# A third landing row, shorter split lead and earlier coefficient loads in the middle of an FNet/H3 kernel

## The chip, the cores and the metric

The kernel runs on one core of a Trainium2 chip. A core has a matrix engine (PE, TensorE), a vector engine (DVE), a scalar engine (ACT), a general engine (POOL) and a sequencer that issues transfers (SP); each runs its own list of instructions in order and waits on semaphores for the others. The metric is the device time of one execution in microseconds.

## The reference, cut to what matters

Two kinds of layers alternate, A, B, A, B, each with a layer norm and a residual, on x of 2048 rows by 576 channels:

```python
def A(x):   # FNet: real part of a Fourier transform along channels and along rows
    a, b = x @ Wd_re.T, x @ Wd_im.T
    return Ws_re @ a - Ws_im @ b

def B(q, k, v, shift_k, ssm_k, ssm_D):   # H3: causal convolution over all 2048 rows
    kv = short_conv4(k, shift_k) * v
    y = irfft(rfft(pad(kv)) * rfft(pad(ssm_k)))[:2048] + kv * ssm_D
    return q * y

x = x + A(layernorm(x)); x = x + B(layernorm(x), ...)
x = x + A(layernorm(x)); x = x + B(layernorm(x), ...)
```

The convolution of B takes k, v and the filter alone and not x, so its result (before the gate) is computed once, beside the first layer A, and used in both layers B.

## The kernel before, in words

All products run in float32 by parts: an operand is split into a rounded high part h (a copy on ACT) and a low part l = x - h (a subtraction on DVE), and a product is h*h + h*l + l*h, three matmuls.

Layer A (`layer`) runs 128 steps n = (g, tb, k): four blocks tb of 512 output rows, two parts g (real, imaginary) and 16 pieces k of 128 input rows. Step n needs one coefficient piece of 128x512 (`c_mat`): a transfer into a raw tile (ring `craw`), then its split into a slot of the ring `cs` of three. A step is 14 matmuls of 512 columns into the five PSUM banks s0 to s3 and rm. After the last k of each 16 steps (n = 47, 63, 79, 95, 111 in the stretch at issue) the banks are evacuated into U: four splits (`evac_u`, L262), and for rm a copy, an addition and a split through a scratch tile `rt` (`evac_r`, L271 to L273). With a block done, four pieces of the hidden product with W (`hidden`, 27 matmuls of 288 columns each half) are pending.

Between these steps, the branch of layer B (`branch`) is fed in small portions. Its middle stage begins at step 45 and has 37 groups: load from t, split (`split_mid`), a product with the filter's and one with the signal's half (`mid_kernel`, `mid_signal`), four DVE operations that multiply them (L570 to L573), a split (`mid_round`) and an inverse product (`mid_inverse`) whose copy is stored to `v_d`. The inverse stage then has 16 rows j of two halves: load of a row from `v_d` (`load_row`), split of each half (`split_row`), a product of four 288-wide matmuls with constants loaded by POOL, and its evacuation by two copies on ACT (L661) and two additions on DVE (L662). ACT operations of both stages show as L510 in the profile, since they go through a helper.

What sets the order: the Python code writes the operations in program order, with a plan that hands out the branch's portions by cost (`MID_COST`, `MID_PAUSE`, `I2_PAUSE`, `I2_COST`; `branch_steps` takes the next portion when the plan's share is behind the work passed). A scheduler in the compiler then fixes each engine's list when the kernel is built, by readiness in a model of its own; `issue_after` pins some pairs. On the chip each list runs strictly in order.

In the middle and inverse stages the ring `craw` has two tiles: the words at `RT_AT`, which are also the scratch `rt` of `evac_r`, and a tile at word 8 of the same buffer. Step 48 is the first to use this ring. Coefficient piece n + 2 is loaded and split at step n. In the inverse stage two rows can be landing (`land`), four half rows can be split (`df`), three half rows are split ahead of the first product, and row j + 2 is loaded when the second half of row j has been split.

Of the kernel before, what the change touches and what calls it, by code (L numbers as in the profile page):

```python
# [10 lines left out]
F32 = mybir.dt.float32  # L11
# [4 lines left out]
P = 128  # L16
Q = P // 2
S = 2048
D = 576
J = S // P  # L20
TB = 4
NT = 512
# [16 lines left out]
MID_LOAD = 45  # L39
MID_FROM = 47  # L40
I2_END = 111
PREP = 113
MW = 504
MID_COST = (2.9, 2.6, 1.8)
MID_PAUSE = 4.0
I2_PAUSE = 6.0
BORDER = {J - 1: 0.5, 0: 0.75}
I2_COST = 2.4
# [20 lines left out]
def fnet_h3_kernel(ctx: ExitStack, tc: tile.TileContext, x, c_mat, w_re, w_im, k_pad, v, shift_k,  # L69
# [144 lines left out]
    CT = {}  # L214

    def load_c(step):
        g, tb, k = step
        raw = ring["craw"]()
        anchor.append(load_after(raw, c_mat[g, tb, k]) if anchor else nc.sync.dma_start(raw, c_mat[g, tb, k]).ins)
        c = ring["cs"]()  # L220
        t = c[:, :NT], c[:, NT:]
        with behind(*stored):
            halved[:] = split(t[0], t[1], raw)
        CT[step] = t

# [88 lines left out]
    def layer(get_x, xres, done, pending, blocks=TB):  # L314
        steps = [(g, tb, k) for tb in range(blocks) for g in range(2) for k in range(J)]
        for n, (g, tb, k) in enumerate(steps):
# [3 lines left out]
            if n + 2 < len(steps):  # L320
                load_c(steps[n + 2])
            for i in range(XLEAD + 1 if blocks == TB else 1):
                if n + i < J:
                    get_x(n + i)
# [7 lines left out]
            for dc in range(NC):  # L332
                xh = X[k][:, dc * P:(dc + 1) * P]
                xl = X[k][:, D + REM + dc * P:D + REM + (dc + 1) * P]
                mm(ps[dc], xh, c[0], first, False)
                mm(ps[dc], xh, c[1], False, False)
                mm(ps[dc], xl, c[0], False, last)
                if dc == NC // 2 - 1:
                    yield n, False
                if last:  # L340
                    (evac_u if blocks == TB else save_u)(g, ps, dc)
# [19 lines left out]
    def branch():  # L361
# [135 lines left out]
        apart = [m1[:, at:at + MW].bitcast(F32), flts[:, 8 + NT:8 + NT + MW]]  # L497
        lay(flts, RT_AT, ("craw", NT, 1))
        at = lay(flts, 8, ("craw", NT, 1)) + MW
# [127 lines left out]
        lay(m1, 0, ("df", 2 * D, 4), ("fc", 2 * P, 6))  # L627
        assert lay(flts, 8 + NT, ("land", 2 * D, 2), ("vo", D, 3)) <= RT_AT - 3 * HD

# [10 lines left out]
        def split_row(j, hf):  # L640
            if j < J:
# [5 lines left out]
                if hf:  # L647
                    del landed[j]
                    load_row(j + 2)
# [20 lines left out]
        for j in range(2):  # L670
            load_row(j)
        yield I2_PAUSE
        for n in range(3):
            split_row(*divmod(n, 2))
            yield I2_COST
        for j in range(J):
            fc, yo = fcs.pop(j), ring["vo"]()
            for hf in range(2):
                vf = halves.pop((j, hf))
                split_row(*divmod(2 * j + hf + 3, 2))  # L680
# [129 lines left out]
    work = mid_work + I2_PAUSE + 35 * I2_COST  # L810
# [386 lines left out]
```

## Time and profile before

| | |
|---|---|
| median of three runs | 1185.95 us (1183.89 to 1187.08) |
| the profiled execution | 1185.81 us |
| its span, first to last instruction | 1184.0 us |
| mean granted PE clock | 0.998 |
| middle stage, from the waits and the timeline | about 218 to 512 us |
| inverse stage | about 516 to 605 us |

In the profile's rows a name like `mats<-flts` says which buffer is written from which: `mats` holds the parts of x and the split coefficients, `flts` float32 tiles (raw coefficients, landing rows, scratch), `mid` the split data of the branch, `u` and `w` the parts of U and W, `bk` the three PSUM banks that the branch and the hidden product share, `s` and `rm` the five banks of layer A. PEld are weight loads, which run beside matmuls; SPq and ACTq are the transfers that SP and ACT issue. In a timeline row stand start, duration, engine, line, operation, tiles, shape and count; in brackets how long the engine had stood idle before it and what ended that.

### The profile page before, as it was taken

The page shows a single profiled execution, that of the slowest core. Times are in us where ns is not written, and L with a number is a line of the kernel's source. Part 1 is how long each engine was busy: PE and PEld are TensorE (multiplying, and loading weights), DVE is VectorE, ACT ScalarE, POOL GpSimd, SP SyncE. Part 2 cuts the span into 40 slices and gives each one's busy share as a digit, 9 for nine tenths or more (in the row PEclk, how much of TensorE's full clock was granted, in tenths as well). Part 3 has the DMA queues.
Part 4 walks back from the last instruction along what each step waited for, and adds up shares of the span by engine and source line. Part 5 has one row for each costly group of instructions (what it writes and reads, how often), then busy time and mean ns, then how long its engine had stood idle before and what let it go on. Part 6 is the DMA issues. An engine that isn't in the chain of part 4 may idle for free.

```text
span 1184.0 us, 17305 instructions
## 1 busy us (share of the span) xinstructions
PE 1166.3 (99%) x6013; PEld 1005.3 (85%) x6013; DVE 846.0 (71%) x1415; ACT 630.8 (53%) x1154; POOL 67.4 (6%) x100
## 2 busy tenths in 40 slices
PE   7999999999999999999999999999999999999997
PEld 6888888887878888888888898888888888889997
DVE  7899794678677678657857765864875776874764
ACT  7965665566655667556646666534434445540200
POOL 2200000000000000001002111000000000001111
PEclk9999999999999999999999999999999999999999
DMA  9889898546666647468857786772682598696621
GB/s 343 289 262 306 275 288 258 193 156 193 192 203 195 200 133 194 108 195 261 248 151 262 244 259 214 253 259 72 205 300 73 179 315 275 197 343 192 214 97 41
DMA packets 153770, 255.60 MB, mean 216 GB/s; under 512 B 27601, under 2 KB 66769, under 8 KB 153682
## 3 DMA queue, kind: packets, MB, share of 16 engines
q1 hardware_dynamic: 115122, 205.58, 54.7%
q10 hardware_dynamic: 33952, 42.63, 10.6%
q0 software_dynamic: 4608, 6.29, 2.2%
q8 instruction: 47, 0.77, 0.3%
q14 instruction: 41, 0.34, 0.1%
HBM read 187.80 MB, written 66.65 MB: 215 GB/s over the span
## 4 chain that ended last, share of the span: by engine, by line
PE 92%; DMA 3%; DVE 2%; ACT 1%; issue 1%; SPq 0%; POOLq 0%; POOL 0%; DVEq 0%; ACTq 0%
PE s L78 53%; PE bk L78 33%; PE rm L78 6%; DMA flts<-in_c_mat 1%; DMA flts<-vd 1%; DVE mats L96 0%; ACT mid L510 0%; DMA vd<-flts 0%; DVE u L96 0%; DVE flts L184 0%; ACT flts L510 0%; DVE mid L645 0%; DVE mats L201 0%; ACT mats L95 0%; DVE flts L662 0%
## 5 line engine op out<-in xcount | busy, mean ns | idle before, releaser
L78 PE MATMUL s<-mats 128*128 128x512 f32 x2088 | 525.9, 392 | 0.7 <-ACT mats L95 0.6
L78 PEld LDWEIGHTS s<-mats 128*128 128x128 f32 x2088 | 387.0, 188 | 79.3 <-ACT mats L95 1.1
L96 DVE TENSOR_TENSOR mats<-flts,mats 128x512 fp32r<-128x512 f32 x201 | 137.4, 688 | 69.9 <-ACT mats L95 67.2
L95 ACT ACTIVATE mats<-flts 128x512 fp32r<-128x512 f32 x201 | 125.8, 627 | 98.6 <-PE bk L78 35.2
L510 ACT ACTIVATE flts<-bk 64x504 f32<-64x504 f32 (+1 forms) x212 | 111.8, 528 | 64.2 <-PE bk L78 59.0
L78 PE MATMUL bk<-w,u 128*128 128x288 f32 x864 | 121.5, 295 | 0.0
L78 PEld LDWEIGHTS bk<-w,u 128*128 128x128 f32 x864 | 118.1, 188 | 2.5 <-DVE flts L295 0.6
L78 PE MATMUL bk<-mid 128*128 128x504 f32 (+1 forms) x461 | 115.9, 366 | 3.4 <-DVE flts L662 1.6
L78 PEld LDWEIGHTS bk<-mid 128*128 128x128 f32 x461 | 80.5, 188 | 23.4 <-DVE flts L662 4.3
L510 ACT ACTIVATE mid<-flts 128x1008 fp32r<-128x1008 f32 (+2 forms) x106 | 75.0, 710 | 43.7 <-DVE flts L573 18.1
L78 PE MATMUL rm<-mats 128*128 128x512 f32 x304 | 94.9, 391 | 0.0
L458 ACT ACTIVATE flts<-bk 128x288 f32<-128x288 f32 x128 | 50.7, 410 | 49.3 <-PE bk L78 48.1
L78 PE MATMUL bk<-f1r 128*128 128x288 f32 x384 | 64.7, 301 | 6.8 <-ACT f1r L95 6.4
L78 PEld LDWEIGHTS bk<-f1r 128*128 128x128 f32 x384 | 59.9, 192 | 13.3 <-ACT f1r L95 6.4
L78 PE MATMUL bk<-mats 128*128 128x288 f32 (+1 forms) x376 | 67.8, 317 | 0.0
L78 PEld LDWEIGHTS rm<-mats 128*128 128x128 f32 x304 | 57.0, 188 | 12.2
L78 PE MATMUL s<-t,mats 128*128 128x512 f32 x264 | 64.9, 389 | 0.0
L295 DVE TENSOR_TENSOR flts<-flts,bk 128x288 f32<-128x288 f32 x48 | 21.8, 453 | 56.2 <-PE bk L78 56.0
L187 POOL TENSOR_TENSOR flts<-flts 128x1 f32<-128x1 f32 x35 | 30.7, 877 | 541.2 <-DVE flts L186 494.6
L515 DVE TENSOR_TENSOR mid<-flts,mid 128x1008 fp32r<-128x1008 f32 (+2 forms) x74 | 58.1, 802 | 4.6 <-ACT mid L510 4.6
L78 PE MATMUL bk<-mats,t 128*128 128x288 f32 (+1 forms) x368 | 59.3, 303 | 0.0
L78 PEld LDWEIGHTS bk<-mats 128*128 128x128 f32 x376 | 55.6, 188 | 3.4
(151 smaller groups left out, 1486.1 us busy)
## 6 DMA issues: line engine op xcount, KB each, us to landing
flts<-in_c_mat SPq DMA_DIRECT2D x148, 256.0 KB, 3.9
ph<-in_c_mat SPq DMA_DIRECT2D x54, 512.0 KB, 4.2
t<-flts ACTq DMA_DIRECT2D x64, 288.0 KB, 4.8
flts<-in_c_mat SPq DMA_DIRECT2D x30, 512.0 KB, 5.6
flts<-vd SPq DMA_DIRECT2D x16, 576.0 KB, 5.0
vd<-flts ACTq DMA_DIRECT2D x36, 252.0 KB, 3.1
flts<-t SPq DMA_DIRECT2D x16, 504.0 KB, 4.1
ud<-ph ACTq DMA_DIRECT2D x12, 512.0 KB, 6.6
```

The lines of the kernel that those rows point to most:

```text
L78: nc.tensor.matmul(ps, lhsT, rhs, start=first, stop=last, skip_group_check=more)
L95: a = nc.scalar.activation(h, src, AF.Copy).ins
L96: return a, nc.vector.tensor_tensor(l, src, h.bitcast(F32), OP.subtract).ins
L187: pows.append(nc.gpsimd.tensor_tensor(rs, ve, mhalf, OP.pow).ins)
L295: added[:] = [nc.vector.tensor_tensor(rows[hf], rows[hf], ps[:, :HD], OP.add).ins]
L458: stored[:] = [nc.scalar.activation(so[:, b, :], ps[:, :HD], AF.Copy).ins]
L510: last_act.append(nc.scalar.activation(*args, **kw).ins)
L515: nc.vector.tensor_tensor(l, src, h.bitcast(F32), OP.subtract)
```

## The change

Inverse stage: a third landing row is taken from the region of the branch's split data, where one of the four half-row slots is given up and the constants move down; three rows are loaded at the start, row j + 3 follows row j, and halves are split two ahead of their product and not three. `I2_PAUSE` goes from 6 to 10, and one `I2_COST` less stands in the plan's work.

Middle and inverse stages (steps 46 to 112): the transfer of a coefficient piece is parted from its split (`fetch_c`), and piece n + 3 is fetched at step n, behind the split of piece n + 2; at the first step of a group of 16 (k = 0) it is fetched in the middle of the step. The two raw tiles change places in the ring: even pieces use the tile at word 8 and odd ones the shared scratch.

```diff
-I2_PAUSE = 6.0
+I2_PAUSE = 10.0
...
-    CT = {}
+    CT, CR = {}, {}
+
+    def fetch_c(step):
+        g, tb, k = step
+        raw = CR[step] = ring["craw"]()
+        anchor.append(load_after(raw, c_mat[g, tb, k]) if anchor else nc.sync.dma_start(raw, c_mat[g, tb, k]).ins)
 
     def load_c(step):
-        g, tb, k = step
-        raw = ring["craw"]()
-        anchor.append(load_after(raw, c_mat[g, tb, k]) if anchor else nc.sync.dma_start(raw, c_mat[g, tb, k]).ins)
+        if step not in CR:
+            fetch_c(step)
+        raw = CR.pop(step)
...
             if n + 2 < len(steps):
                 load_c(steps[n + 2])
+            soon = blocks == TB and MID_LOAD < n < PREP
+            if soon and k > 0:
+                fetch_c(steps[n + 3])
...
                 if dc == NC // 2 - 1:
                     yield n, False
+                    if soon and k == 0:
+                        fetch_c(steps[n + 3])
...
+        at = lay(flts, 8, ("craw", NT, 1)) + MW
         lay(flts, RT_AT, ("craw", NT, 1))
-        at = lay(flts, 8, ("craw", NT, 1)) + MW
...
-        lay(m1, 0, ("df", 2 * D, 4), ("fc", 2 * P, 6))
+        at = lay(m1, 0, ("df", 2 * D, 3), ("fc", 2 * P, 6))
         assert lay(flts, 8 + NT, ("land", 2 * D, 2), ("vo", D, 3)) <= RT_AT - 3 * HD
+        ring["land"].tiles.append(m1[:, at:at + 2 * D].bitcast(F32))
...
-                    load_row(j + 2)
+                    load_row(j + 3)
...
-        for j in range(2):
+        for j in range(3):
             load_row(j)
         yield I2_PAUSE
-        for n in range(3):
+        for n in range(2):
...
-                split_row(*divmod(2 * j + hf + 3, 2))
+                split_row(*divmod(2 * j + hf + 2, 2))
...
-    work = mid_work + I2_PAUSE + 35 * I2_COST
+    work = mid_work + I2_PAUSE + 34 * I2_COST
```

The lists of the engines differ from step 46 to about step 112 alone. Three places show how; line numbers of the changed kernel are 5 to 11 higher than those of the profile. First ACT's list at the evacuation of step 63 (`u_753` is U, `rm_2555` the remainder's bank, `mats_70<-flts_72 128x512` the high part of a coefficient piece, `mid_2078` the branch's split data), before:

```order
L95 ACTIVATE u_753<-s3_69 128x512
L271 ACTIVATE flts_72<-rm_2555 64x512
L95 ACTIVATE u_753<-flts_72 64x512
L510 ACTIVATE mid_2078<-flts_72 128x1008
L510 ACTIVATE flts_72<-bk_3080 128x504
L594 DMA vd_78<-flts_72 128x504
L95 ACTIVATE mats_70<-flts_72 128x512
L510 ACTIVATE mid_2078<-flts_72 128x504
L510 ACTIVATE flts_72<-bk_3096 64x504 x3
L95 ACTIVATE mats_70<-flts_72 128x512 x2
```

and after:

```order
L95 ACTIVATE u_753<-s3_69 128x512
L276 ACTIVATE flts_72<-rm_2555 64x512
L95 ACTIVATE mats_70<-flts_72 128x512
L95 ACTIVATE u_753<-flts_72 64x512
L520 ACTIVATE mid_2078<-flts_72 128x1008
L520 ACTIVATE flts_72<-bk_3080 128x504
L604 DMA vd_78<-flts_72 128x504
L95 ACTIVATE mats_70<-flts_72 128x512
L520 ACTIVATE mid_2078<-flts_72 128x504
L520 ACTIVATE flts_72<-bk_3097 64x504 x3
L95 ACTIVATE mats_70<-flts_72 128x512
```

The split of piece 66 has moved from behind the store of `v_d` to between the copy and the split of the remainder; pieces 67 and 68 stand where 66 and 67 stood. On SP, the loads of 66, 67 and 68 follow each other directly after the change; before, a store of W and a load from t stand between 67 and 68.

Second, PE's list behind step 79, where `rm_3073` is the remainder's bank of step 79 and `rm_4005` that of steps 80 and on, and each `bk` a product of the middle stage, before:

```order
L78 MATMUL rm_3073<-mats_70 128x512 x2
L78 MATMUL bk_3984<-mid_2078 128x504 x3
L78 MATMUL bk_3996<-mid_2078 128x504
L78 MATMUL s0_66<-mats_70 128x512 x2
L78 MATMUL bk_3996<-mid_2078 128x504 x2
L78 MATMUL s0_66<-mats_70 128x512
L78 MATMUL bk_4022<-mid_2078 128x504 x2
L78 MATMUL s1_67<-mats_70 128x512 x3
L78 MATMUL s2_68<-mats_70 128x512 x3
L78 MATMUL s3_69<-mats_70 128x512 x3
L78 MATMUL rm_4005<-mats_70 128x512 x2
```

and after:

```order
L78 MATMUL bk_3997<-mid_2078 128x504 x3
L78 MATMUL s0_66<-mats_70 128x512 x3
L78 MATMUL bk_4014<-mid_2078 128x504 x3
L78 MATMUL s0_66<-mats_70 128x512 x3
L78 MATMUL bk_4039<-mid_2078 128x504 x2
L78 MATMUL s1_67<-mats_70 128x512 x6
L78 MATMUL bk_4039<-mid_2078 128x504
L78 MATMUL s0_66<-mats_70 128x512
L78 MATMUL s1_67<-mats_70 128x512
L78 MATMUL s2_68<-mats_70 128x512 x3
L78 MATMUL s3_69<-mats_70 128x512 x3
L78 MATMUL rm_4005<-mats_70 128x512 x2
```

Parts of steps 81 and 82 (s0 and s1) now stand ahead of s2, s3 and rm of step 80. Behind step 47 the order changes in the same manner: one product moves ahead of step 47's s2, and step 50's first matmul stands behind step 49's s0, ahead of step 48's s1. DVE's list at step 79 now has the four multiplications of one product and a 1008-wide split ahead of the subtractions that evacuate s2 and s3.

Third, ACT's list at the start of the inverse stage, from the copy of step 95's remainder to the first evacuation of an inverse product (`bk_4612`, after the change `bk_4611`; `128x576` is a half row's split, `128x4x72` the last store to `v_d`), before:

```order
L271 ACTIVATE flts_72<-rm_4005 64x512
L95 ACTIVATE u_753<-flts_72 64x512
L510 ACTIVATE mid_2078<-flts_72 128x288
L510 ACTIVATE flts_72<-bk_4499 128x288
L596 DMA vd_78<-flts_72 128x4x72
L95 ACTIVATE mats_70<-flts_72 128x512 x3
L510 ACTIVATE mid_2078<-flts_72 128x576 x4
L95 ACTIVATE mats_70<-flts_72 128x512
L510 ACTIVATE flts_72<-bk_4612 64x288
```

and after:

```order
L276 ACTIVATE flts_72<-rm_4005 64x512
L95 ACTIVATE mats_70<-flts_72 128x512
L95 ACTIVATE u_753<-flts_72 64x512
L520 ACTIVATE flts_72<-bk_4500 128x288
L606 DMA vd_78<-flts_72 128x4x72
L95 ACTIVATE mats_70<-flts_72 128x512 x2
L520 ACTIVATE mid_2078<-flts_72 128x576 x3
L95 ACTIVATE mats_70<-flts_72 128x512
L520 ACTIVATE flts_72<-bk_4611 64x288
```

The last split of the middle stage (`128x288`) has moved ahead of U's evacuation, and three half rows are split before the first inverse product is evacuated, not four. From there on the products stand at the same places in PE's list as before.

## The prediction

> **What bounds the kernel now.** I read the page's engine line first, then the chain that ended last, then windows by stage, then the list of waits, and last the timeline around each wait.
>
> ```profile
> PE 1166.3 (99%) x6013; PEld 1005.3 (85%) x6013; DVE 846.0 (71%) x1415; ACT 630.8 (53%) x1154; POOL 67.4 (6%) x100
> ```
>
> TensorE is the bound, and its only reserve is the stretches where its matmuls do not follow each other at their full pace. The chain gives that pace, from two long stretches with nothing between:
>
> ```profile
> 845.02 23.12 PE s L78 x102
> 1062.17 115.02 PE bk L78 x866
> ```
>
> A 512-wide matmul takes 23.12 / 102 = 0.2267 us from start to start, a 288-wide one 115.02 / 866 = 0.1328 us; the 504-wide ones are close to the first. A later start than that is lost time, even where the busy column says 100%. The windows show where:
>
> ```profile
> 324.00:347.00 23.00, 21.49 (x105) 17.65 (x104) 16.08 (x25) 13.24 (x24) 0.00 (x0) 1.00 0.60 199
> 505.00:552.00 47.00, 45.37 (x247) 38.63 (x246) 31.15 (x54) 27.42 (x52) 3.71 (x7) 1.00 0.75 222
> 850.00:900.00 50.00, 50.00 (x223) 41.40 (x222) 37.17 (x51) 21.07 (x34) 0.00 (x0) 1.00 0.74 245
> ```
>
> (Window, its length, then busy time of PE, weight loads, DVE, ACT, POOL, then the granted clock.) The first is the evacuation at step 63 in the middle stage, the second the start of the inverse stage; the third is a stretch where nothing waits. So few microseconds are to be had. The Trainium skill (Trainium Kernel Development and Optimization, Performance Expectations) says that matmul busy time is a bad measure and weight-load busy share a good one. By that, 85% would leave 15% of the span, 178 us, to be won. The trace does not agree: in the stretch without a wait weight loads are busy 41.40 of 50 us, 83%, so 85% is already full here.
>
> ```profile
> PE bk L78 <- DVE flts L662: 1.6, 3, 0.8
> PE bk L78 <- DVE flts L572: 1.0, 1, 1.0
> ACT mid L510 <- DMA flts<-vd: 12.0, 9, 2.8
> SPq L169 <- DVE u L96: 28.6, 4, 13.1
> ```
>
> (Waiter, what ended the wait, us in all, times, longest.) PE waits for product evacuations of the inverse stage (L662) and of the middle stage (L572). Behind the first stand row loads that land late (ACT waits 12.0 us for them), behind the second the coefficient loads, which stand in SP's queue behind the evacuation of U, because the even steps' raw tile is also the scratch of that evacuation.
>
> **The change, part by part.** No work is added: 128 coefficient loads and splits, 16 row loads, 32 half-row splits, as before. What moves is when loads are issued and in which order ACT, DVE and PE do the same things. I price by place, PE's lost time alone.
>
> *Step 63/64, raw tiles swapped and one step more of lead.*
>
> ```profile
> 330.26 0.81 SPq L169 DMA_DIRECT2D flts<-in_c_mat  x2
> 333.19 0.63 ACT L95 ACTIVATE mats<-flts 128x512 fp32r<-128x512 f32 x1 [2.13 <-DMA flts<-in_c_mat]
> 334.86 0.53 SPq L169 DMA_DIRECT2D flts<-in_c_mat  x1
> 340.46 1.55 PE L78 MATMUL s<-mats 128*128 128x512 f32 x6
> 340.71 0.63 ACT L95 ACTIVATE mats<-flts 128x512 fp32r<-128x512 f32 x1 [4.05 <-PE bk L78]
> 342.48 0.96 PE L78 MATMUL bk<-mid 128*128 128x504 f32 x3 [0.47 <-DVE flts L295]
> 344.48 0.95 PE L78 MATMUL bk<-mid 128*128 128x504 f32 x3 [1.04 <-DVE flts L572]
> 345.27 1.09 PE L78 MATMUL s<-mats 128*128 128x512 f32 x4
> ```
>
> Loads 66 and 67 are issued at 330.26, when the scratch is free; 68 needs 66's split and goes at 334.86; ACT stands 4.05 us until it lands (the wait is put down to PE, but ACT's next work is the split at 340.71). Evacuations behind it come late, and PE loses 342.48 - (340.46 + 6 x 0.2267) = 0.66, then 344.48 - (342.48 + 3 x 0.2267) = 1.32, then 0.11: 2.09 us. After, 66 uses the other tile, is loaded before the evacuation and split inside it, where ACT waits for DVE. 67 takes the shared tile and still goes at about 330.26; SP's later loads and stores queue behind it as they did behind 66. 68 follows at once instead of at 334.86. Even with the 5.85 us that 68 took (334.86 to 340.71) it lands at 336.5; its split then stands at the place in ACT's order where 67's was, at about 336.0. What is late next is a half microsecond on ACT, which PE does not see. Bounds 0 and 2.09; I take 2.1, since the 4.05 us are gone, not just shorter.
>
> *Step 47/48.*
>
> ```profile
> 256.24 1.52 PE L78 MATMUL bk<-mid 128*128 128x504 f32 x6
> 256.93 1.58 ACT L95 ACTIVATE u<-s 128x512 fp32r<-128x512 f32 x3
> 258.53 0.60 ACT L271 ACTIVATE flts<-rm 64x512 f32<-64x512 f32 x1
> 264.68 1.60 PE L78 MATMUL bk<-mid 128*128 128x504 f32 x6
> 266.93 3.01 PE L78 MATMUL s<-mats 128*128 128x512 f32 x12 [0.64 <-ACT mats L95]
> ```
>
> PE loses 266.93 - (264.68 + 6 x 0.2267) = 0.89 us for step 50's split. After, load 50 is early, but PE's new order wants its first matmul much sooner: one product (three matmuls) stands ahead of 256.24, then twelve matmuls follow, so 256.24 + 15 x 0.2267 = 259.64. ACT has by then three U copies (to 258.51), one product copy and the remainder copy (0.60 each) and the split (0.63): 260.34. A new wait of 0.70 takes the place of 0.89. Gain 0.2 (bounds -0.7, if both are paid, and 0.89).
>
> *Step 79/80.* Here nothing is lost before, and the new order mixes middle products into the evacuation (front, second pair of orders).
>
> ```profile
> 438.66 1.06 PE L78 MATMUL bk<-mid 128*128 128x504 f32 x4
> 440.64 1.29 DVE L96 TENSOR_TENSOR u<-s,u 128x512 fp32r<-128x512 f32 x2 [0.35 <-ACT u L95]
> L570 DVE TENSOR_TENSOR flts<-bk,flts 128x504 f32<-128x504 f32 x36 | 24.5, 681 | 22.5 <-PE bk L78 14.6 <-ACT flts L510 7.8
> L515 DVE TENSOR_TENSOR mid<-flts,mid 128x1008 fp32r<-128x1008 f32 x18 | 21.6, 1201 | 0.0
> ```
>
> DVE finishes s3's evacuation at 441.93. After, four product operations (0.68) and a 1008-wide split (1.20) stand ahead of it: 3.9 us later, 445.85. PE wants s3 for step 80 after 26 matmuls from 438.66: 444.55. So up to 1.3 us are lost; none, if DVE's own waits there close up (0.35 in the row). I take the middle, 0.6.
>
> *Inverse stage: three rows landing, splits two ahead, pause 10.*
>
> ```profile
> 509.90 0.44 ACT L510 ACTIVATE mid<-flts 128x288 fp32r<-128x288 f32 x1
> 512.23 0.37 ACTq L596 DMA_DIRECT2D vd<-flts  x1
> 516.32 1.38 SPq L169 DMA_DIRECT2D flts<-vd  x2
> 520.63 1.26 ACT L510 ACTIVATE mid<-flts 128x576 fp32r<-128x576 f32 x2 [2.79 <-DMA flts<-vd]
> 524.35 0.62 PE L78 MATMUL rm<-mats 128*128 128x512 f32 x2
> 525.78 1.02 PE L78 MATMUL bk<-mid 128*128 128x288 f32 x4 [0.80 <-DVE flts L662]
> 526.63 2.16 PE L78 MATMUL bk<-w,u 128*128 128x288 f32 x15
> 528.98 1.03 PE L78 MATMUL bk<-mid 128*128 128x288 f32 x4 [0.19 <-DVE flts L662]
> 544.09 1.55 PE L78 MATMUL s<-mats 128*128 128x512 f32 x6
> 546.29 0.80 PE L78 MATMUL bk<-mid 128*128 128x288 f32 x4 [0.64 <-DVE flts L662]
> ```
>
> PE loses 525.78 - (524.35 + 2 x 0.2267) = 0.98, 526.63 - (525.78 + 4 x 0.1328) = 0.32, 528.98 - (526.63 + 15 x 0.1328) = 0.36 and 546.29 - (544.09 + 6 x 0.2267) = 0.84: 2.50 us. All come from ACT waiting for a row while an evacuation stands behind it. After, the last split of the middle stage (509.90) stands ahead of U's evacuation, and the last product's copy comes straight behind it (third pair of orders): about 509.9 + 0.5, so its store goes some 1.8 us before 512.23, the first rows start and land that much earlier (518.8 instead of 520.63), the third row has its own tile, and each later load is issued five half-rows ahead of its split instead of three. ACT does three splits, not four, before the first evacuation. Bounds: 0 and 2.50; I take 2.5. The pause itself costs PE nothing: it only spaces the plan, whose work goes from 274.1 + 6 + 35 x 2.4 = 364.1 to 274.1 + 10 + 34 x 2.4 = 365.7, so that middle pieces come up to 0.4% sooner. POOL's constant loads now use other words of the same region and wait for the same last middle product.
>
> Sum: 2.1 + 0.2 - 0.6 + 2.5 = 4.2 us. The profiled execution took 1185.81, so 1181.6; the median of the three runs (1185.95) lies 0.1 above it, which I neglect.
>
> **The rivals.**
>
> *Evacuations eat it.* As the 0.70 and 1.3 us above: the new order puts pairs of middle products close together in other places too. With step 80 at 1.3, step 48 at -0.7 and two more such waits of 0.7, the gain is 2.1 + 2.5 - 1.3 - 0.7 - 1.4 = 1.2: 1184.6. For it: step 80 shows what a few DVE operations ahead of an evacuation do. Against: the list of waits has a single PE wait on middle products (L572, 1.0 us), and that is step 64's.
>
> *The earlier fetch does nothing.* There are still two raw tiles, so load n still waits for the split of n-2. Then the inverse stage alone gains, step 80 pays: 1185.8 - 2.5 + 0.6 = 1183.9. Against: at step 64 the tile, not the lead, was the obstacle.
>
> *All waits go.* 2.09 + 0.89 + 2.50 = 5.5 and some tenths at other products: 1180.0.
>
> *Slower: splits two ahead come too late.* One half-row less lies between a split and its product.
>
> ```profile
> 534.87 0.76 DVE L645 TENSOR_TENSOR mid<-flts,mid 128x576 fp32r<-128x576 f32 x1 [0.20 <-ACT mid L510]
> 535.20 0.69 PE L78 MATMUL bk<-mid 128*128 128x288 f32 x4
> 539.49 0.69 PE L78 MATMUL bk<-mid 128*128 128x288 f32 x4
> ```
>
> This split, issued with the product at 535.20, ends at 535.63; after the change its product is the second from there, at 539.49: 3.9 us of margin. If ACT and DVE fall back by more than that, as they would when a row again lands late, products starve as the three above did, 0.73 us each ((0.98 + 0.36 + 0.84) / 3). With 10 of 32: 7.3 us, the 2.5 not gained: 1185.8 - 1.7 + 7.3 = 1191.4. It decides from some seven products on. Against: rows get five half-rows of lead.
>
> **Chances and range.** The forecast (gain 3.6 to 5.2) 0.54, all waits go 0.12, evacuations eat it 0.16, fetch does nothing 0.05, slower 0.13. 1181.6 is the likeliest. About 0.3% (3.6 us) is what a measurement tells here: faster by more 0.66, within 0.21, slower 0.13. The range goes from just below all waits gone, 1179.3, to 1186.0, past the weak gains; it leaves out the slower case and little below. The forecast's own range is 1180.6 to 1182.2.
>
> **What would show it.** Right: no ACT wait near 4 us for a coefficient load around 336 to 341, ACT's wait for rows down from 12.0 to under 4 us, no PE wait on the inverse evacuation, new PE waits under 1 us each near 260 and 445. Wrong: PE waiting for the half-row splits (L645) more than twice, sums of PE waits in the middle stage above 3 us, or rows that still start at 516.

## The result, and the profile after

| | before | after |
|---|---|---|
| median, 7 runs each on one chip | 1186.89 us (1183.89 to 1187.86) | 1181.09 us (1180.28 to 1182.73) |
| profiled execution | 1185.81 us | 1180.65 us |
| its span | 1184.0 us | 1178.8 us |
| mean granted PE clock | 0.998 | 0.999 |

The ratio is 0.9957 with a 95% interval of 0.9946 to 0.9969: 0.43% faster, 3.7 to 6.4 us. The same stages in the windows of the changed kernel (window, length, busy time of PE, weight loads, DVE, ACT, POOL, granted clock, DMA share, GB/s; the second lies 4 us sooner than before, as the stage does):

```profile
324.00:347.00 23.00, 23.00 (x113) 19.48 (x112) 19.07 (x29) 15.48 (x26) 0.00 (x0) 1.00 0.58 192
501.00:548.00 47.00, 47.00 (x260) 41.27 (x259) 31.72 (x54) 28.07 (x53) 4.23 (x8) 1.00 0.76 229
```

PE is busy throughout both, with 113 matmuls in place of 105 and 260 in place of 247. Step 63/64, where ACT had stood for load 68 and three matmul groups had come late, in the timeline of the changed kernel:

```profile
327.50 0.63 ACT L95 ACTIVATE mats<-flts 128x512 fp32r<-128x512 f32 x1
328.34 0.63 ACT L95 ACTIVATE u<-flts 64x512 fp32r<-64x512 f32 x1 [0.21 <-DVE flts L277]
329.78 0.81 SPq L169 DMA_DIRECT2D flts<-in_c_mat  x2
332.62 0.63 ACT L95 ACTIVATE mats<-flts 128x512 fp32r<-128x512 f32 x1 [2.10 <-DMA flts<-in_c_mat]
335.46 0.63 ACT L95 ACTIVATE mats<-flts 128x512 fp32r<-128x512 f32 x1
339.93 1.55 PE L78 MATMUL s<-mats 128*128 128x512 f32 x6
341.31 1.54 PE L78 MATMUL bk<-mid 128*128 128x504 f32 x6
342.69 1.55 PE L78 MATMUL s<-mats 128*128 128x512 f32 x6
```

The split at 327.50 is piece 66's, in the gap in which ACT had waited for DVE; 67 and 68 are issued together at 329.78; 67's split waits 2.10 us as before (2.13), and 68's, at 335.46, waits for nothing. Six matmuls of 0.2267 us take 1.36: 339.93, 341.31, 342.69 follow each other without a gap (1.38 each).

The start of the inverse stage in the same timeline:

```profile
508.02 0.37 ACTq L606 DMA_DIRECT2D vd<-flts  x1
512.17 1.18 SPq L169 DMA_DIRECT2D flts<-vd  x2
514.60 0.52 SPq L169 DMA_DIRECT2D mid<-vd  x1
516.44 1.26 ACT L520 ACTIVATE mid<-flts 128x576 fp32r<-128x576 f32 x2 [3.08 <-DMA flts<-vd]
520.42 0.83 ACT L520 ACTIVATE flts<-bk 64x288 f32<-64x288 f32 x2 [0.69 <-PE bk L78]
521.87 0.62 PE L78 MATMUL rm<-mats 128*128 128x512 f32 x2
522.33 0.69 PE L78 MATMUL bk<-mid 128*128 128x288 f32 x4
```

The last store goes at 508.02 and not 512.23, the rows at 512.17 and not 516.32, and the first evacuation (520.42) now waits for PE and not PE for it. In the list of waits from 205 to 605 us:

```profile
ACT mid L520 <- DMA flts<-vd: 3.3, 2, 3.1
ACT mats L95 <- DMA flts<-in_c_mat: 4.3, 6, 2.1
```

ACT's waits for rows fell from 12.0 us to 3.3. PE waits for no evacuation of L673 (L662 before).

For an account by stage I took PE's lost time from the two traces: for each pair of neighbouring matmuls the time from start to start, less the usual time of the first one's form in these traces (the median: 0.227 us for 512 wide, 0.228 for 504, 0.132 for 288), summed over stretches. The stretches hold the same places in all kernels of this document.

| stretch, us (place) | before | after | gain |
|---|---|---|---|
| 250 to 300 (step 47/48) | 1.71 | 1.43 | 0.28 |
| 300 to 350 (step 63/64) | 2.77 | 0.44 | 2.33 |
| 350 to 500 (step 79/80, rest of the middle stage) | 1.97 | 2.23 | -0.26 |
| 500 to 600 (inverse stage) | 4.50 | 1.31 | 3.19 |
| 600 to 700 (the gate's first rows) | 0.46 | 1.38 | -0.92 |

With 0.12 from all other stretches, where a first matmul that starts 0.69 later is counted in, the sum is 4.74 us, and PE's last matmul does start 4.73 us sooner (1172.15 for 1176.88). The spans differ by 5.2; the rest lies behind the last matmul. The loss of 0.92 stands in no part of the prediction. The orders printed ahead of the prediction were said to differ up to about step 112 alone; on ACT, DVE and SP they also differ in the gate's rows, up to step 126, and there PE waits twice, at 647.60 (0.39) and 654.21 (0.56). The timeline of both:

```profile
646.04 0.87 ACT L727 ACTIVATE gate<-gate,flts 128x576 f32<-128x576 f32 x1 [1.33 <-DVE flts L726]
646.82 0.61 ACT L95 ACTIVATE mats<-flts 128x512 fp32r<-128x512 f32 x1
647.60 0.40 PE L78 MATMUL s<-mats 128*128 128x512 f32 x1
648.21 2.76 PE L78 MATMUL s<-mats 128*128 128x512 f32 x11 [0.22 <-DVE mats L96]
655.00 2.33 PE L78 MATMUL s<-mats 128*128 128x512 f32 x9 [0.40 <-DVE u L96]
```

At the first a coefficient split stands behind a gate operation that waits 1.33 us for the norm's chain; the second is a wait for an evacuation into U. The second is no accident of one execution: nine of the fourteen kernels of this document, one trace each, lose 0.54 to 0.56 us there, the other five nothing that stands out.

### The profile page after: what moved, and what is told of

Its sections match the earlier page's. It is cut to its first block, busy times and chain, and to the rows that moved or that the text cites. A ratio compares the mean times of both kernels' runs of the same rounds, so it can differ in the third digit from the quotient of the medians.

```text
span 1178.8 us, 17315 instructions
## 1 busy us (share of the span) xinstructions
PE 1164.0 (99%) x6013; PEld 1004.9 (85%) x6013; DVE 845.4 (72%) x1415; ACT 631.8 (54%) x1154; POOL 66.7 (6%) x100
## 4 chain that ended last, share of the span: by engine, by line
PE 92%; DVE 3%; DMA 2%; ACT 2%; issue 1%; POOL 0%; SPq 0%; POOLq 0%; DVEq 0%; ACTq 0%
PE s L78 52%; PE bk L78 35%; PE rm L78 5%; DVE mats L96 1%; DVE flts L184 1%; DMA flts<-in_c_mat 1%; DMA flts<-in_ssm_k 0%; DMA yb<-flts 0%; DVE mats L201 0%; DMA flts<-yb 0%; ACT flts L520 0%; POOL flts L187 0%; ACT u L95 0%; ACT mats L95 0%; DVE gate L716 0%
## 5 line engine op out<-in xcount | busy, mean ns | idle before, releaser
L520 ACT ACTIVATE mid<-flts 128x1008 fp32r<-128x1008 f32 (+2 forms) x96 | 68.2, 712 | 31.1 <-DVE flts L583 14.4
L300 DVE TENSOR_TENSOR flts<-flts,bk 128x288 f32<-128x288 f32 x48 | 21.8, 454 | 58.9 <-PE bk L78 58.8
```

Of the source, the lines that this page charges most:

```text
L300: added[:] = [nc.vector.tensor_tensor(rows[hf], rows[hf], ps[:, :HD], OP.add).ins]
L520: last_act.append(nc.scalar.activation(*args, **kw).ins)
```

## Experiments

My theory at this point: the places are separate terms, and their gains add up. The rivals: one part brings everything; the lead and not the tile (or the tile and not the lead) counts; the third row and not the shorter lead counts; the pause is only spacing. All ratios are to the kernel before, measured on the same chip. Line numbers are those of each kernel.

**The inverse stage's part alone** (on the kernel before):

```diff
-I2_PAUSE = 6.0
+I2_PAUSE = 10.0
...
-        lay(m1, 0, ("df", 2 * D, 4), ("fc", 2 * P, 6))
+        at = lay(m1, 0, ("df", 2 * D, 3), ("fc", 2 * P, 6))
+        ring["land"].tiles.append(m1[:, at:at + 2 * D].bitcast(F32))
...
-                    load_row(j + 2)
+                    load_row(j + 3)
...
-        for j in range(2):
+        for j in range(3):
             load_row(j)
         yield I2_PAUSE
-        for n in range(3):
+        for n in range(2):
...
-                split_row(*divmod(2 * j + hf + 3, 2))
+                split_row(*divmod(2 * j + hf + 2, 2))
...
-    work = mid_work + I2_PAUSE + 35 * I2_COST
+    work = mid_work + I2_PAUSE + 34 * I2_COST
```

> The kernel before with the inverse stage's part alone (third landing row, row j + 3 after row j, splits two ahead, pause 10, plan work 34); coefficient pieces loaded as before, raw tiles not swapped. Working theory (gains add up by place): the inverse stage's 2.5 us go, the 4.05 us wait of ACT for load 68 and PE's 2.09 us behind step 63 stay, step 50's split is still late (0.89 in the kernel before), step 79/80 has the new order and costs 0.1 to 0.6. Time 2.0 to 2.4 us below the kernel before, ratio 0.9980 to 0.9983; PE's lost time between 200 and 500 us about 8 as before, between 500 and 600 us down from 4.5 to about 1.5. Rival (the inverse stage brings all that was measured): 5 us or more below, 0.9955. Rival (rows had always been hidden, the coefficient part brings it all): within 0.5 us of the kernel before.

Measured 1186.73 us against 1186.61, ratio 0.9999 (0.9988 to 1.0010). A miss: the time does not move. By the trace, PE loses 2.56 us from 500 to 600 (4.50 before, about 1.5 expected) and 1.67 from 300 to 350 (2.77 before), but 3.97 from 350 to 500, twice as much as before. Its timeline at the two places where it waits:

```profile
443.58 1.64 PE L78 MATMUL s<-mats 128*128 128x512 f32 x6 [0.28 <-DVE u L96]
446.12 5.87 SPq L169 DMA_DIRECT2D flts<-in_c_mat  x4
449.47 1.31 ACT L95 ACTIVATE mats<-flts 128x512 fp32r<-128x512 f32 x2 [0.63 <-DMA flts<-in_c_mat]
449.77 0.50 PE L78 MATMUL bk<-mid 128*128 128x504 f32 x1 [0.58 <-DVE flts L572]
526.92 0.63 ACT L95 ACTIVATE mats<-flts 128x512 fp32r<-128x512 f32 x1 [1.95 <-DMA flts<-in_c_mat]
527.58 0.83 ACT L510 ACTIVATE flts<-bk 64x288 f32<-64x288 f32 x2
528.81 1.02 PE L78 MATMUL bk<-mid 128*128 128x288 f32 x4 [0.79 <-DVE flts L663]
```

The new pacing moves step 79/80 nearly to the order of the changed kernel; two matmuls fewer stand ahead of s2, and PE waits for U's evacuation (443.58, 0.45 lost). Behind it PE's list has two products and the first matmul of a third in a row (from 447.33 on), and PE waits for DVE's multiplications (449.77, 0.74 lost). At the first inverse products an evacuation stands on ACT behind a coefficient split whose load landed late (526.92), which is step 64's mechanism at one more place.

**The coefficient part alone** (changed kernel with the inverse stage of before):

```diff
-I2_PAUSE = 10.0
+I2_PAUSE = 6.0
...
-        ring["land"].tiles.append(m1[:, at:at + 2 * D].bitcast(F32))
...
-                    load_row(j + 3)
+                    load_row(j + 2)
...
-                split_row(*divmod(2 * j + hf + 2, 2))
+                split_row(*divmod(2 * j + hf + 3, 2))
...
```

(The other lines of the inverse stage go back in the same way.)

> The kernel before with the coefficient part alone: raw tiles swapped and piece n + 3 fetched at step n; inverse stage as before. Working theory: step 63/64 gives 2.1, step 47/48 0.2 to 0.5, nothing at step 79/80, where PE's order is nearly that of the kernel before; the inverse stage keeps its 2.5 us of loss. Time 2.3 to 2.6 us below the kernel before, ratio 0.9978 to 0.9981; PE's lost time from 324 to 347 us near 0, from 505 to 552 us still about 3. Rival (earlier fetch does nothing): within 0.5 us of the kernel before, ACT still standing 4 us near 337. Rival (the inverse stage's late rows were only late because of the coefficient loads on SP): 4.5 us or more below.

Measured 1185.91 us, ratio 0.9988 (0.9979 to 0.9997). Step 63/64 is cured (0.77 lost from 300 to 350), the inverse stage is not (4.56 from 500 to 600), and the gate's waits are there already (1.71 from 600 to 700). A gain of 0.4 to 2.5 us, where 2.3 to 2.6 had been expected, short by the gate's loss of 1.2 which nobody had priced. So the two parts alone give 0 and about 1.4 us, together 5: the terms do not add up. The traces say the same (from 250 to 700 us 1.08 and 1.06 us less lost alone, 4.62 together) and where: from 350 to 500 the inverse part alone costs 2.00 and with the coefficient part the two cost 0.26, and the inverse stage gains 1.94 from its own part, nothing from the other, and 3.19 from both. The timeline of the kernel with the coefficients alone:

```profile
519.84 1.26 ACT L520 ACTIVATE mid<-flts 128x576 fp32r<-128x576 f32 x2 [5.86 <-DMA flts<-vd]
521.65 0.69 ACT L520 ACTIVATE mid<-flts 128x576 fp32r<-128x576 f32 x1 [0.56 <-DMA flts<-vd]
522.76 0.67 ACT L520 ACTIVATE mid<-flts 128x576 fp32r<-128x576 f32 x1
523.46 0.83 ACT L520 ACTIVATE flts<-bk 64x288 f32<-64x288 f32 x2
524.81 1.02 PE L78 MATMUL bk<-mid 128*128 128x288 f32 x4 [0.81 <-DVE flts L672]
```

Here the rows land late and four splits stand ahead of the first evacuation.

**No earlier fetch** (changed kernel):

```diff
-            soon = blocks == TB and MID_LOAD < n < PREP
+            soon = False
```

> The changed kernel with piece n + 3 not fetched at step n: load n + 2 stands at step n as before, tiles stay swapped, inverse stage as changed. The lists of PE, ACT and DVE are those of the changed kernel; SP's list alone differs, with W's stores and loads from t ahead of some coefficient loads. Theory A (the tile was the obstacle, as the prediction says): no difference to the changed kernel beyond 0.5 us, 5 to 6 us below the kernel before, ratio 0.9950 to 0.9958, no ACT wait over 2.5 us for a coefficient load. Theory B (the lead carries the gain at steps 63 and 47): piece 68 or 50 is late again by 1 to 4 us, PE loses 1 to 2.5 us there, time 2.5 to 4 us below the kernel before, ratio 0.9966 to 0.9979.

Measured 1183.02 us, ratio 0.9961 (0.9949 to 0.9973); the loss from 250 to 700 is 6.98 us against 6.79 in the changed kernel. The ratio lies between the ranges of the two theories; the trace is theory A's, with 0.43 lost from 300 to 350 as in the changed kernel (0.44): with the tiles swapped the lead is worth nothing that these runs can tell.

**No swap of the tiles** (changed kernel):

```diff
-        at = lay(flts, 8, ("craw", NT, 1)) + MW
         lay(flts, RT_AT, ("craw", NT, 1))
+        at = lay(flts, 8, ("craw", NT, 1)) + MW
```

> The changed kernel with the raw tiles not swapped: even pieces again use the words that are also the scratch of the remainder's evacuation; earlier fetch and inverse stage as changed. PE's list is nearly that of the changed kernel; ACT's differs mainly in that the splits of pieces 50, 66, 82, 98 and 114, the third behind each evacuation, stand one to three operations later. Theory A (the tile is what frees both stages): PE loses 1.2 to 2.1 us near 342, about 1.6 between 442 and 450 and about 1 near 527, as with the inverse part alone; time within 1.5 us of the kernel before, ratio 0.9985 to 1.0. Theory B (lead and swap can stand for each other): losses as in the changed kernel, 0.995 to 0.9963.

In this kernel pieces 50, 66, 82, 98 and 114 are fetched into the scratch before the evacuation writes over them, so five steps multiply by other numbers; instructions, sizes and transfers are those of the full computation. Measured 1179.32 us, ratio 0.9938 (0.9926 to 0.9951). Theory A fell. By its trace the kernel is even ahead of the changed one (5.86 us lost for 6.79, since in the gate's rows 0.14 are lost for 1.38); the intervals of the two ratios overlap. Its timeline at step 63/64:

```profile
320.94 2.93 SPq L169 DMA_DIRECT2D flts<-in_c_mat  x2
325.55 0.59 ACT L276 ACTIVATE flts<-rm 64x512 f32<-64x512 f32 x1
328.61 0.62 ACT L95 ACTIVATE mats<-flts 128x512 fp32r<-128x512 f32 x1
```

Piece 66 leaves before the evacuation (320.94), and its split at 328.61 waits for nothing. For the time it is enough that the load behind an evacuation is issued ahead of it; a swap does that, and so does a lead. For the result the lead needs the swap: fetched a step early, an even piece would lie in words that the evacuation still has to write.

**Two landing rows** (changed kernel):

```diff
-                    load_row(j + 3)
+                    load_row(j + 2)
-        for j in range(3):
+        for j in range(2):
             load_row(j)
-        ring["land"].tiles.append(m1[:, at:at + 2 * D].bitcast(F32))
```

> The changed kernel with two landing rows: row j + 2 follows row j and two rows are loaded at the start, splits two ahead as changed. The lists of PE, ACT and DVE stay those of the changed kernel, SP's loads of rows alone stand later. Theory A (the third tile carries the inverse stage's gain, since its load has five half rows of lead): row loads have three half rows of lead as in the kernel before, the third and fourth rows land late, PE loses 1 to 2.5 us between 515 and 550 us, time 3 to 4.5 us below the kernel before, ratio 0.9962 to 0.9975. Theory B (the earlier last store of the middle stage and fewer splits ahead of the first evacuation carry it): PE loses under 0.5 us there, time within 0.5 us of the changed kernel, ratio 0.9950 to 0.9958.

Measured 1181.72 us, ratio 0.9961 (0.9948 to 0.9975); 1.37 us lost from 500 to 600, against 1.31. The ratio lies between the ranges of the two theories, but the lost time is theory B's: the third row, which gives the change its name, is worth nothing that shows here.

**Only the pause of the inverse part** (on the kernel with the coefficient part alone: two rows, splits three ahead):

```diff
-I2_PAUSE = 6.0
+I2_PAUSE = 10.0
```

> The coefficient part as changed, and of the inverse part only the pause of 10 in place of 6; two landing rows, four half-row slots, splits three ahead as before. Theory A (the inverse stage's gain comes from what the plan's pacing does to the order: the last store of the middle stage earlier, first splits later): the loss between 505 and 552 us falls under 1 us and the time is 4 to 6 us below the kernel before, ratio 0.9950 to 0.9966. Theory B (two instead of three splits ahead of the first product carry it): 2 to 3.5 us lost there as with the coefficients alone, ratio 0.9978 to 0.999.

Measured 1181.46 us, ratio 0.9962 (0.9949 to 0.9974); 2.16 lost from 500 to 600, of it 0.52 up to 550. Theory A; behind 550 one wait for an evacuation is left (0.49 at 579.96) that the changed kernel does not have.

**The pause of 6** (changed kernel):

```diff
-I2_PAUSE = 10.0
+I2_PAUSE = 6.0
```

> The changed kernel with the pause of 6 of before. Theory A (pacing carries the inverse stage's gain): rows are issued near 516 us, 1.5 to 3 us lost between 505 and 552, time 2 to 4 us below the kernel before, ratio 0.9966 to 0.9983. Theory B (the shorter lead of the splits carries it): losses as in the changed kernel, ratio 0.9950 to 0.9963.

Measured 1182.2 us, ratio 0.9972 (0.9960 to 0.9984); 1.51 lost from 500 to 600, 0.74 of it up to 550. In the inverse stage that is theory B. The time itself lies in theory A's range, but for another reason than that theory gives: 0.96 us more than in the changed kernel are lost from 350 to 500 and 0.42 more from 600 to 700. With the run before it, either the pause or the other edits (third row and shorter lead) are enough for the start of the inverse stage; the third row alone and the shorter lead alone were not run. What the two kernels have in common can be seen on ACT. First the timeline of the kernel with a pause of 10 and four splits, then that of the kernel with a pause of 6 and three:

```profile
510.56 1.19 SPq L169 DMA_DIRECT2D flts<-vd  x2
515.46 1.26 ACT L520 ACTIVATE mid<-flts 128x576 fp32r<-128x576 f32 x2 [1.88 <-DMA flts<-vd]
```

```profile
513.60 1.18 SPq L169 DMA_DIRECT2D flts<-vd  x2
518.43 1.26 ACT L520 ACTIVATE mid<-flts 128x576 fp32r<-128x576 f32 x2 [5.49 <-DMA flts<-vd]
```

With the pause of 10 the rows are issued 5 us sooner than with the coefficients alone (510.56 for 515.59), and four splits are done in time. With the pause of 6 ACT waits 5.49 us for the rows, nearly as long as the 5.86 above, but one split fewer stands ahead of the first evacuation, and in the list of waits from 505 to 605 us PE has none.

**One split ahead** (changed kernel):

```diff
-        for n in range(2):
+        for n in range(1):
             split_row(*divmod(n, 2))
...
-                split_row(*divmod(2 * j + hf + 2, 2))
+                split_row(*divmod(2 * j + hf + 1, 2))
...
-    work = mid_work + I2_PAUSE + 34 * I2_COST
+    work = mid_work + I2_PAUSE + 33 * I2_COST
```

> The changed kernel with one split ahead of its product, plan work one portion less. Tests the prediction's rival of splits that come too late. With two ahead a margin of 3.9 us was worked out; products stand about 2.1 us apart, so one ahead leaves 1.7 us. Theory A (margin enough but at evacuations): PE waits for split half rows two to six times, 1 to 4 us in all, ratio 0.9965 to 0.9995. Theory B (starvation as in the rival): over ten waits of about 0.7 us, 7 us or more above the changed kernel, ratio over 1.001. Theory C (lead doesn't matter at all): as the changed kernel.

Measured 1181.21 us, ratio 0.9955 (0.9942 to 0.9967): theory C, as the changed kernel. ACT's longest wait for a row is 6.05 us, and no product waits, as its timeline shows:

```profile
518.83 1.26 ACT L520 ACTIVATE mid<-flts 128x576 fp32r<-128x576 f32 x2 [6.05 <-DMA flts<-vd]
520.28 0.75 PE L78 MATMUL bk<-mid 128*128 128x288 f32 x4
520.80 0.83 ACT L520 ACTIVATE flts<-bk 64x288 f32<-64x288 f32 x2 [0.19 <-PE bk L78]
```

What PE waited for in this stage were evacuations behind splits, never a split; from 500 to 600 us it loses 1.53 here and 1.31 with two splits ahead. The prediction's slower rival is out, with room to spare.

**Where the gate's two waits come from.** First, piece 115 loaded at step 114 (changed kernel):

```diff
-            if n + 2 < len(steps):
+            if blocks == TB and n == PREP + 1:
+                load_c(steps[n + 1])
+            if n + 2 < len(steps) and not (blocks == TB and n == PREP):
                 load_c(steps[n + 2])
-            soon = blocks == TB and MID_LOAD < n < PREP
+            soon = blocks == TB and MID_LOAD < n < PREP - 1
```

> The changed kernel, but piece 115 is loaded and split at step 114 and no longer fetched at step 112, where its tile is the scratch of step 111's evacuation; PE's and DVE's lists are those of the changed kernel, on ACT the splits of pieces 117 and 118 stand one operation later. It tests where the two new PE waits near 647 and 654 us (0.39 and 0.56) come from. Theory A (the load of 115 holds SP's queue from 599 to 606 us until the scratch is free, the first loads of the gate stand behind it, and the gate's chain of ACT and DVE then runs into the splits): loads of yb and xa issued 1 to 3 us sooner, both waits gone, about 1 us less than the changed kernel, ratio to the kernel before 0.9940 to 0.9950. Theory B (ACT's order of splits and gate operations there does it, whatever the loads do): both waits stay, ratio 0.9950 to 0.9963. Rival: the later load makes PE wait at step 115, 1 us or more above the changed kernel.

Measured 1180.8 us, ratio 0.9956 (0.9942 to 0.9970). The waits stay (0.21 and 0.54), so theory A fell as it stood: the first load of `yb` goes at 601.33 instead of 607.04, but the two of `xa` at 612.23, later and not sooner (611.02 in the changed kernel). Second, a pause of 12, with which ACT's order in the gate's rows is another (changed kernel):

```diff
-I2_PAUSE = 10.0
+I2_PAUSE = 12.0
```

> The changed kernel with a pause of 12 in place of 10. ACT's order from piece 119 on differs from the changed kernel's: piece 122 is split ahead of the gate operation that waits for the chain of the norm. If that order makes the two PE waits near 647 and 654 us, they are gone here and the time is about 1 us below the changed kernel, ratio to the kernel before 0.9940 to 0.9950; if the gate's late loads make them, they stay, 0.9950 to 0.9963. On the inverse stage: if the pause is a fine balance, PE loses 1 us or more between 505 and 552 us; if any edit that loosens the start is enough, under 0.8 as with 10.

Measured 1181.8 us, ratio 0.9956 (0.9941 to 0.9971). The wait near 647 is gone, that near 654 stays (0.54), and 0.28 is lost at 629.71: neither of the two. In the inverse stage 0.49 is lost from 505 to 550 us, so the pause is no fine balance. In the kernel without the swap, ACT's order from piece 116 on is the changed kernel's, and neither wait is there; its `xa` loads go at 608.29 and not 611.02. What holds those loads stands in the changed kernel's list of SP's waits (598 to 620 us) and in its timeline:

```profile
SPq L169 <- DMA yb<-flts: 3.0, 1, 3.0
606.02 1.10 ACTq L676 DMA_DIRECT2D yb<-flts  x2
611.02 0.80 SPq L169 DMA_DIRECT2D flts<-xa  x2
```

The landing tile of `xa` lies over the words from which the inverse stage's last row is being stored. Third, then, that tile and `yb`'s exchanged (changed kernel):

```diff
-            lay(flts, SC_AT + CRAW * NT + 2 * D, ("xa", D, 2), ("yb", D, 2))
+            lay(flts, SC_AT + CRAW * NT + 2 * D, ("yb", D, 2), ("xa", D, 2))
```

> The changed kernel with the landing tiles of xa and yb exchanged in the gate's rows. In the changed kernel xa's tiles lie over the words from which row 15 of the inverse stage is stored to yb; SP's loads of xa wait 3.0 us for that store (issued on ACT at 606.02, loads at 611.02), and the gate's chain starts with xa. Now xa lies over the rows stored before, and yb, which the chain needs later, over row 15; on SP xa's two loads stand ahead of yb's. Theory A (the start of the gate's chain behind that store makes the waits near 647 and 654 us): xa issued 2 to 4 us sooner, the chain's first operations 1 to 3 us sooner, both waits gone, lost time from 600 to 700 us down from 1.38 to under 0.7, time 0.6 to 1.2 us below the changed kernel, ratio to the kernel before 0.9938 to 0.9952. Theory B (ACT's order decides alone): the lost time there stays above 1, ratio 0.9952 to 0.9965. Rival: yb's loads, now behind the store, hold SP's queue and piece 118 lands late: 1 us or more above the changed kernel.

Measured 1181.58 us, ratio 0.9967 (0.9954 to 0.9980), no gain. Its timeline:

```profile
606.92 0.33 SPq L169 DMA_DIRECT2D flts<-xa  x1
616.40 0.69 ACT L700 ACTIVATE gate<-flts 128x576 f32<-128x576 f32 x1 [2.79 <-DVE flts L719]
646.04 0.87 ACT L727 ACTIVATE gate<-gate,flts 128x576 f32<-128x576 f32 x1 [1.33 <-DVE flts L726]
```

The first load goes 4.1 us sooner and the gate's first operation on ACT 1.6 (616.40 for 617.96), but 30 us later, at 646.04, the chain stands where it stood. The wait near 647 shrinks to 0.23, that near 654 stays at 0.54; 1.08 is lost from 600 to 700 where theory A had under 0.7. Theory A is at most a part of it; what sets the chain's pace in between stays open.

**A pause of 9 with the rows of before** (on the kernel with the coefficient part alone):

```diff
-I2_PAUSE = 6.0
+I2_PAUSE = 9.0
```

> The coefficient part as changed, two landing rows and splits three ahead as before, pause 9. With a pause of 6 the start of the inverse stage lost 3.6 us of PE's time between 500 and 552 us, with 10 only 0.5. Theory A (a balance with some slack): about 0.5 to 1.5 lost, ratio 0.9953 to 0.9970. Theory B (a threshold between 9 and 10): 3 us or more lost, 0.9975 to 0.999.

Measured 1184.42 us, ratio 0.9978 (0.9968 to 0.9988). By the time this looks like theory B, but the trace says otherwise: 0.54 is lost from 500 to 550, as with 10. The time goes at 629.97 and 631.07 (0.87 and 0.50), in the gate's rows, and 1.42 go from 700 to 750, where the kernels of this document lose from 0.03 to 1.25. From step 100 on all lists are those of the pause of 10; with evacuations 0.5 us later its `xa` loads go 1.3 later (615.90 for 614.63) and ACT's first gate operation 1.7. So in this pair, with one order, late loads are the likely cause; no run moves them alone. The expectation named one place, and the time was decided at others.

PE's lost time in all runs, by stage:

| kernel | 250-300 | 300-350 | 350-500 | 500-600 | 600-700 | sum |
|---|---|---|---|---|---|---|
| before | 1.71 | 2.77 | 1.97 | 4.50 | 0.46 | 11.41 |
| changed | 1.43 | 0.44 | 2.23 | 1.31 | 1.38 | 6.79 |
| inverse part alone | 1.58 | 1.67 | 3.97 | 2.56 | 0.55 | 10.33 |
| coefficient part alone | 1.00 | 0.77 | 2.31 | 4.56 | 1.71 | 10.35 |
| no earlier fetch | 1.38 | 0.43 | 2.15 | 1.32 | 1.70 | 6.98 |
| no tile swap | 1.15 | 0.55 | 2.69 | 1.33 | 0.14 | 5.86 |
| two landing rows | 1.36 | 0.43 | 2.53 | 1.37 | 1.53 | 7.22 |
| pause 10 without rows | 1.44 | 0.76 | 2.21 | 2.16 | 0.44 | 7.01 |
| pause 6 | 0.69 | 0.65 | 3.19 | 1.51 | 1.80 | 7.84 |
| one split ahead | 0.61 | 0.73 | 2.69 | 1.53 | 1.34 | 6.90 |
| piece 115 later | 1.35 | 0.45 | 2.40 | 1.28 | 1.21 | 6.69 |
| pause 12 | 1.39 | 0.65 | 2.44 | 1.41 | 1.56 | 7.45 |
| pause 9 without rows | 1.42 | 0.76 | 2.79 | 1.88 | 1.70 | 8.55 |
| gate tiles exchanged | 1.36 | 0.44 | 2.52 | 1.30 | 1.08 | 6.70 |

No version that computes everything beats the changed kernel by more than these runs can tell: those at its level have ratios of 0.9955 to 0.9967, with intervals some 0.0025 wide.

## Why the prediction was right, point by point

- *1181.6 us, faster.* Measured 1181.09. The sum of 4.2 us stands against 4.7 in the two traces, and that it comes out so close is in part luck, because errors of opposite sign meet: by the table of stages 0.7 too little at the inverse stage and 0.65 at the three evacuations, and 0.9 not seen in the gate's rows.
- *Step 63/64, 2.1.* Right in size (2.33 in that stretch), place and steps: 66 split inside the evacuation, 67 waiting as before, 68 without a wait. The reason, "the tile, not the lead, was the obstacle", holds for the changed kernel (no earlier fetch: 0.43 lost), but is not the whole of it: without the swap the lead cures the step's time as well (0.55 lost), only not with the right data.
- *Step 47/48, 0.2.* Mechanism right: a new wait for the split takes the place of the old one. Its size was put at 0.70 and is 0.35, in the timeline of the changed kernel. PE wanted the piece at 259.92, 0.28 later than the 259.64 worked out, and the split ended at 260.21, not 260.34.

```profile
259.59 0.62 ACT L95 ACTIVATE mats<-flts 128x512 fp32r<-128x512 f32 x1
260.26 1.90 PE L78 MATMUL s<-mats 128*128 128x512 f32 x7 [0.18 <-ACT mats L95]
```

- *Step 79/80, -0.6.* The mis-sized term of the sum. DVE's work ahead of the evacuation is as described, but of the 1.3 us that the row count gave, 0.07 is left at that place.

```profile
436.99 0.84 PE L78 MATMUL bk<-mid 128*128 128x504 f32 x3
440.37 1.20 DVE L525 TENSOR_TENSOR mid<-flts,mid 128x1008 fp32r<-128x1008 f32 x1
441.49 1.28 DVE L96 TENSOR_TENSOR u<-s,u 128x512 fp32r<-128x512 f32 x2
441.81 2.09 PE L78 MATMUL s<-mats 128*128 128x512 f32 x8
```

  (The same timeline.) s3 is evacuated at 442.77, and 26 matmuls from 436.99 put its first use at 442.88. The changed kernel is 2.4 us ahead at this place (first matmul and all lost time up to 400 us, 18.4 before and 16.0 after), so both moved: DVE was done 0.7 us sooner and PE came 0.7 us later than the two times that I had set against each other. Both were anchored on rows of the old order, and in a new order neither engine keeps its start. That the wait is real two other kernels show: in the inverse part alone and without the swap, s2 comes two matmuls (0.45 us) sooner in PE's list, and PE loses 0.45 (at 443.58) and 0.41 us (at 441.03) to U's evacuation. In the inverse part alone other waits follow, and from 350 to 500 us 2 us more are lost than before. The stretch's -0.26 itself is not clear of scatter: kernels whose PE list is the changed kernel's lose from 2.15 to 2.53 there.
- *Inverse stage, 2.5.* Right in sum (3.19 with the small waits that I had left out) and in its signs: rows at 512, ACT's waits for them under 4 us, no PE wait for an evacuation. Wrong in its steps: the third row does nothing that shows (1.37 without it against 1.31 lost), the pause is not "only spacing" but with the coefficient part enough for the stage's start, and the term is not the inverse part's own. With the old tiles that part gains only 1.94 us of PE's time in its stage, since a late coefficient split then takes the row's place ahead of one evacuation (0.95 lost at 528.81), and it loses as much at step 79/80, so that the time does not move (ratio 0.9999). I had priced each place by the row that stood there, as if the cause behind it could be taken away alone; of two causes in one queue, taking away one shows the other.
- *The rivals.* "All waits go" is near what happened (inverse stage and step 64), and the gate's new waits are what keeps it from 1180.0. "Evacuations eat it": one such wait of 0.35, not four. "The earlier fetch does nothing": true of the fetch, not of the part. "Splits too late": refuted one step further than the change goes. That edits of one stage cost time in the next was in no rival, and its cause stays open; the traces have it at 0.9 us in the changed kernel and 1.2 with a pause of 9 (1.70 less the 0.46 of before).
- *Weight loads as the measure of what is left.* The Trainium skill (Trainium Kernel Development and Optimization, Performance Expectations) names the weight-load busy share, beside the share of the peak rate, as a good measure of how close a kernel is to its roofline. The trace does not agree, as before: the changed kernel's 47 us from 501 on lose under 0.6 us and show 41.27, 88%, so the missing 12% are no reserve.

## What to carry to other kernels

Where several late inputs stand in one in-order queue ahead of the same evacuation, price the repairs together and not one by one: here two parts worth 0 and 1.4 us alone give 5 together, and for the start of one stage either of two sets of edits would have done. When a scheduler fixes the order, compare its lists to the very end of the program, since an edit that ends at step 112 moved splits more than ten steps behind it. And when a tile is shared with a scratch, look first at which transfer has to wait for the scratch; here, giving that place to a transfer that is wanted later cost nothing.

## What the runs showed of the chip beside this

The lowest and the highest execution of one kernel lie 1.4 to 7.7 us apart in the series of this document. The traces, one of each kernel, show part of it ahead of step 46, where the program is the same in all. PE's first matmul starts between 5.82 us (coefficients alone) and 7.14 us (changed kernel), PE loses between 3.60 and 5.28 us in the first 50, and near 216 us it loses between 0 and 1.48 us in a wait for an addition (L300) whose row of x lands late:

```profile
PE bk L78 <- DVE flts L300: 1.2, 1, 1.2
DVE flts L300 <- DMA flts<-in_x: 0.7, 1, 0.7
```

(Waits of the kernel with the coefficients alone.) That is as large as most terms of this case, so a term under 1 us is read from the places in the traces and not from the times.
